# One pair of heads of the first batch: query by query instead of key by key, in another order of work

## The chip, the cores and the metric

The program runs on one core of a Trainium2 chip. The metric is the time of one execution in microseconds (us) on the device; of several executions the median is given. A profiled execution adds a trace: every instruction of the five engines (PE for matmuls, with PEld for its weight loads; DVE, ACT and POOL for element-wise work; SP, which issues the DMA transfers), with its start and duration.

## The reference

Clustered attention feeds a layer with a rational activation. A query may attend to a key only where both have the same nearest of 16 centroids; the mask is exact, so the assignment has to be as well.

```python
B, H, S, D = q.shape                       # 4, 8, 768, 64
q_assign = np.argmax(np.einsum('bhsd,hcd->bhsc', q_n, c_n), axis=-1)
k_assign = np.argmax(np.einsum('bhsd,hcd->bhsc', k_n, c_n), axis=-1)
mask = q_assign[:, :, :, None] == k_assign[:, :, None, :]
scores = np.where(mask, scale * np.matmul(q, k.transpose(0, 1, 3, 2)), -1000000000.0)
attn = np.exp(scores - np.max(scores, axis=-1, keepdims=True))
attn = attn / (np.sum(attn, axis=-1, keepdims=True) + 1e-09)
x = np.matmul(attn, v)                     # to [3072, 512]: tokens by heads
h = x @ w_in                               # 512 -> 2048
P = a[0] + a[1] * h + a[2] * h * h + a[3] * h * h * h
Q = 1.0 + np.abs(b[0]) * np.abs(h) + np.abs(b[1]) * h * h
out = (P / (Q + 1e-6)) @ w_out             # 2048 -> 512
```

## The kernel before

Matmul operands are split into two 16-bit parts, and three products of the parts are summed; this holds for the scores, for attention times `v`, and for both matrices of the layer. The weights arrive as 64-bit numbers and are taken apart in `weights` (lines 503 to 632): ACT, DVE and POOL work on 32 chunks of 128 x 512, in the first 200 us.

The heads are done in pairs, four pairs for each of the four batches, 768 tokens in six tiles of 128. `prep` (line 883) loads `q` and `k` of a pair, scales and splits them, assigns clusters and turns the parts by DMA. Then there are two forms of attention.

*Key by key* (`attend_keys`, line 1264), for the pairs named in `KEYMAJOR`. It needs the maximum of each query's scores first: twelve score tiles (line 1286; a bank of 128 queries by 768 keys, four matmuls) are reduced on DVE to `top` (line 1295). `parts` (lines 1302 to 1312) writes the maxima, split in three, into spare rows of the second query operand, which is turned once more by DMA. Then the scores are made a second time with the keys as rows: tiles `z` (line 1330, six matmuls), from which the matmul itself has subtracted the maximum; ACT's exponential writes them to `at`. `at` is at once the right operand of attention times `v` (`px`, line 1349, in 32 bit) and of the sums (line 1355). Six small instructions for a block of 256 queries (`rw`, lines 1368 to 1400: logarithm, exponential, a Newton step, `spread` by PE at line 1383, a copy, the product) divide by the sums and round to `x`.

*Query by query* (`attend`, line 1143), for all other pairs. For each of twelve tiles of 128 queries by 768 keys: scores (line 1162, four matmuls), a scaling with minimum on DVE (line 1191), the exponential with its sum on ACT, a reciprocal on DVE (line 1210), then the two 16-bit halves `ah` on ACT and DVE (line 1222), which a DMA turns into `at` (line 1229). After two tiles of both heads 36 matmuls make `px` (line 1242), which ACT and DVE round to `x` (line 1258). These pairs need `v` in two halves, `vhi` and `vlo` (line 1138), and the rows for the mask come from a tile `marks` that is turned by DMA, with a copy of the first operand's rows beside it (lines 1026 and 1034).

The layer (`moe`, line 1410) works on blocks of 256 tokens, three for a batch: `ph` (line 1450, twelve matmuls for a column block) needs the `x` of all four pairs of the batch for that block; the rational function runs on ACT, DVE and POOL (lines 1466 to 1564), and `po` (line 1575) multiplies by `w_out`.

Score tiles lie in two banks "s", and in batch 0 every third in the bank "o", which `po` uses later.

Nothing is scheduled at run time. Every step is a numbered operation, and the list `ORDER` says in which order they are given to the engines; each engine, and SP with its DMAs, works through its own steps in that order. Numbers count the steps as the loops at the end of the kernel make them. The choice of the form is one line:

```python
KEYMAJOR = {(b, hp) for b in range(B) for hp in range(kn("km", (4, 0, 0, 0))[b])}
```

Of the kernel before, what the change touches and what calls it, by code (L numbers as in the profile page):

```python
# [57 lines left out]
K = {'mulp': 0.6, 'mulp.3': 0.0, 'a0t': 1.15, 'xn': 14, 'scp': 1, 'vsc': 0.75, 'sup0': 0, 'stk': 2, 'lop': 0, 'mgp': 0, 'rvn': 2, 'at': 3, 'vn': 3, 'ah': 5, 'sqd': 0.0, 'ed': 0.0, 'ed.3': 1.0, 'gld': 0.0, 'gld.3': 1.0, 'sqd.3': 0.0, 'ghd': 0.0, 'sua': 1.0, 'acq': 0.75, 'T1': 1, 'quick': 1}  # L58
# [188 lines left out]
def clustered_attention_moe_kernel(  # L247
# [65 lines left out]
    def kn(name, default=0.0):  # L313
        return K.get(name, default)

# [8 lines left out]
    def kshare(name, b, i):  # L324
        return share(name if f"{name}.{b}" not in K else f"{name}.{b}", i)

# [1339 lines left out]
```

## Time and profile before

| | us |
|---|---|
| median of 3 runs | 929.95 |
| lowest, highest | 928.17, 933.06 |
| the profiled execution | 932.17 |
| its span, first to last instruction | 930.4 |

| engine | busy us | share of the span | instructions |
|---|---|---|---|
| PE | 863.5 | 93% | 7705 |
| DVE | 835.6 | 90% | 1503 |
| ACT | 811.2 | 87% | 1558 |
| POOL | 729.3 | 78% | 771 |

Busy time is the time in which at least one instruction of the engine runs; where records overlap, their durations sum to more. Ends of matmuls are modelled, so a busy PE isn't PE at its peak. In a row of the trace, "128x768 f16<-128x768 f32 x144 | 129.0, 901 | 7.8 <-DVE su" means: 144 instructions of this form, 129.0 us busy, 901 ns each in the mean, and 7.8 us in which the engine was idle just before them, mostly until DVE wrote `su`.

A row of a stretch has start and end, its length, then the busy time and, in brackets, the records of PE, PEld, DVE, ACT and POOL in this order, then the mean granted clock of PE, the busy share of the 16 DMA engines and what they moved in GB/s. Where a stretch is asked for the instructions of one tile alone, an engine that has none is left out: of the three rows 5, the first (`rw`) has all five, the second (`at`) PE, PEld and ACT, the third (`rest`) DVE alone; they hold the four pairs of batch 0 together.

### The profile page before, as it was taken

How to read it: one execution, taken by the hardware profiler on the slowest of the kernel's cores; microseconds unless marked ns; L12 is line 12 of the kernel's file. 1: busy time of each engine (PE TensorE's matmuls, PEld its weight loads, DVE VectorE, ACT ScalarE, POOL GpSimd, SP SyncE). 2: the span in 40 equal slices, each digit the busy share in tenths (PEclk: the TensorE clock that was granted, in tenths of full speed). 3: DMA queues.
4: the chain of work that ended last, by engine and by line, in shares of the span. 5: the costliest groups of instructions: out<-in, count | busy, mean ns of one | idle time of the engine just before them, and what ended most of it. 6: DMA issues, size and time to landing. Idle time of an engine off the chain costs nothing.

```text
span 930.4 us, 20764 instructions
## 1 busy us (share of the span) xinstructions
PE 863.5 (93%) x7705; PEld 581.1 (62%) x7705; DVE 835.6 (90%) x1503; ACT 811.2 (87%) x1558; POOL 729.3 (78%) x771
## 2 busy tenths in 40 slices
PE   1679998988899999999989999999999999999997
PEld 1357665656566666666666766666666675777663
DVE  6789999769989999999999999999999998899986
ACT  5577697989999999999999999999999998886774
POOL 2546789988999999999989988988989996464342
PEclk9989999989999999999999999999999999999999
DMA  7995765796977899998799879896987587501000
GB/s 200 232 249 130 190 193 148 177 230 138 188 133 154 164 161 203 155 167 163 155 162 180 164 135 169 178 188 110 208 150 150 92 165 130 121 2 33 8 24 23
DMA packets 360853, 137.70 MB, mean 148 GB/s; under 512 B 335665, under 2 KB 352049, under 8 KB 360753
## 3 DMA queue, kind: packets, MB, share of 16 engines
q1 hardware_dynamic: 360752, 136.39, 72.0%
q8 instruction: 60, 0.98, 0.4%
q14 instruction: 41, 0.33, 0.1%
HBM read 41.98 MB, written 6.29 MB: 52 GB/s over the span
## 4 chain that ended last, share of the span: by engine, by line
PE 54%; DVE 19%; ACT 9%; POOL 6%; issue 6%; DMA 5%; SPq 1%; ACTq 0%; DVEq 0%; POOLq 0%
PE ph L1450 18%; PE po L1575 18%; PE s L1162 7%; PE px L1242 5%; DVE ah L1222 3%; DVE s L1191 3%; DMA rvm<-in_v_dram 2%; PE s L1286 2%; DVE t L1467 1%; DVE t L1556 1%; ACT s L395 1%; PE px L1349 1%; DVE t L1468 1%; DVE top L1295 1%; PE z L1330 1%
## 5 line engine op out<-in xcount | busy, mean ns | idle before, releaser
L1450 PE MATMUL ph<-x,win 128*128 128x256 f16 x2304 | 273.1, 273 | 6.3 <-DVE t L1468 4.7
L1450 PEld LDWEIGHTS <-win 128*128 128x128 f16 x2304 | 223.2, 98 | 55.3 <-DVE t L1468 8.6
L1575 PE MATMUL po<-wout,s 128*128 128x512 f16 x1008 | 239.3, 379 | 0.7 <-POOL s L1564 0.7
L1191 DVE TENSOR_SCALAR_CACHE_REDUCE s<-s,cc 128x768 f32<-128x768 f32 x144 | 145.9, 1017 | 15.4 <-PE s L1162 14.8
L1575 PEld LDWEIGHTS <-s 128*128 128x128 f16 x1008 | 96.4, 98 | 101.2 <-issue 2.2
L1222 DVE SCALAR_TENSOR_TENSOR ah<-s,su,ah 128x768 f16<-128x768 f32 x144 | 144.9, 1011 | 5.6 <-ACT ah L395 5.3
L395 ACT ACTIVATE ah<-s,su 128x768 f16<-128x768 f32 x144 | 129.0, 901 | 7.8 <-DVE su L1210 7.2
L395 ACT ACTIVATE s<-s,nm 128x768 f32<-128x768 f32 x144 | 126.1, 876 | 7.3 <-DVE s L1191 4.9
L1162 PE MATMUL s<-sk,sq 128*128 128x384 f16 x576 | 117.8, 329 | 8.9 <-DVE ah L1222 7.9
L1516 POOL TENSOR_TENSOR s<-s,u 128x512 f32<-128x512 f32 x84 | 114.4, 1362 | 7.0
L1538 POOL TENSOR_TENSOR s<-s,u 128x512 f32<-128x512 f32 x72 | 99.1, 1378 | 7.0 <-ACT u L395 6.7
L1515 POOL TENSOR_SCALAR s<-u,g 128x512 f32<-128x512 f32 x84 | 69.6, 829 | 36.4 <-ACT u L395 33.6
L1564 POOL TENSOR_TENSOR s<-t,s 128x512 f16<-128x512 f32 x72 | 88.1, 1226 | 8.8 <-ACT s L1560 6.8
L1162 PEld LDWEIGHTS <-sq 128*128 128x128 f16 x576 | 52.2, 98 | 53.7 <-DVE ah L1222 17.9
L1556 DVE SCALAR_TENSOR_TENSOR t<-s,t 128x512 f32<-128x512 f32 x84 | 81.8, 973 | 0.8 <-POOL s L1538 0.5
L1242 PE MATMUL px<-at,vhi 128*64 128x256 f16 x864 | 75.2, 276 | 0.0
L395 ACT ACTIVATE u<-ph,gk 128x512 f32<-128x512 f32 x84 | 57.8, 688 | 9.3 <-PE ph L1450 8.7
L1468 DVE SCALAR_TENSOR_TENSOR t<-t,gk,ph 128x512 f32<-128x512 f32 x84 | 62.8, 748 | 3.0
L395 ACT ACTIVATE t<-ph,gk 128x512 f32<-128x512 f32 x84 | 65.4, 780 | 0.0
L1467 DVE SCALAR_TENSOR_TENSOR t<-ph,gk,t 128x512 f32<-128x512 f32 x84 | 62.1, 739 | 1.1 <-ACT t L395 1.0
L1545 POOL TENSOR_TENSOR t<-t,u 128x512 f32<-128x512 f32 x43 | 57.6, 1340 | 3.6
L1242 PE MATMUL px<-at,vlo 128*64 128x256 f16 x432 | 59.7, 273 | 0.0
(232 smaller groups left out, 1751.3 us busy)
## 6 DMA issues: line engine op xcount, KB each, us to landing
rwi<-in_moe_w_in_dram SPq DMA_DIRECT2D x16, 512.0 KB, 4.1
rwo<-in_moe_w_out_dram SPq DMA_DIRECT2D x16, 512.0 KB, 4.4
rk<-in_k_dram SPq DMA_DIRECT2D x32, 192.0 KB, 3.4
rq<-in_q_dram SPq DMA_DIRECT2D x32, 192.0 KB, 3.7
rvm<-in_v_dram SPq DMA_DIRECT2D x16, 384.0 KB, 3.8
rv<-in_v_dram SPq DMA_DIRECT2D x16, 384.0 KB, 4.1
out_dram<-ob SPq DMA_DIRECT2D x24, 256.0 KB, 2.9
sk<-sk SPq DMA_DIRECT2D x12, 192.0 KB, 3.4
```

The costliest lines, as they stand in the source:

```text
L395: lambda: nc.scalar.activation(out=out(), in_=in_(), func=func, **{a: (x() if callable(x) else x) for a, x in kw.items()}),
L1162: nc.tensor.matmul(sc.ap[:, i, :SH], lhsT=st["q" + x].ap[:, j, t, :], rhs=st["k" + x].ap[:, j, ks, :].rearrange("p t c -> p (t c)"), start ...
L1191: lambda nm=nm, view=view: ts(out=view(), in0=view(), scalar1=cc.ap[:, 0:1], scalar2=None, op0=ALU.mult, op1=ALU.min, accum_out=nm.ap),
L1222: lambda part=part, view=view, su=su: stt(out=part(1), in0=view(), scalar=su.ap, in1=part(0), op0=ALU.mult, op1=ALU.subtract),
L1242: nc.tensor.matmul(px.ap[j * D : (j + 1) * D, :], lhsT=vv.ap[:, j, kt, :], rhs=at[j].ap[:, p_, kt].rearrange("p t c -> p (t c)"), start=(i ...
L1450: nc.tensor.matmul(ph.ap[:, fi * TW : (fi + 1) * TW], lhsT=win[:, wpart, c, f * P : (f + 1) * P], rhs=xs[c].ap[:, xpart], start=(i == 0), ...
L1468: stt(out=t[h].ap, in0=t[h].ap, scalar=col("a1")(), in1=ph.ap, op0=ALU.add, op1=ALU.mult)
L1516: nc.gpsimd.tensor_tensor(out=sv(), in0=sv(), in1=uv(), op=ALU.mult)
L1538: lambda uv=uv, sv=sv: nc.gpsimd.tensor_tensor(out=sv(), in0=sv(), in1=uv(), op=ALU.mult),
L1556: lambda tv=tv, sv=sv: stt(out=tv(), in0=sv(), scalar=2.0, in1=tv(), op0=ALU.subtract, op1=ALU.mult),
L1564: lambda tv=tv, g16=g16, e=(nc.vector if kshare("gld", b, i_) else nc.gpsimd): e.tensor_tensor(out=g16(1), in0=tv(), in1=g16(0), op=ALU.su ...
L1575: nc.tensor.matmul(po[ti].ap, lhsT=g16(gg)[:, c0 : c0 + P], rhs=wout[:, wpart, f, :], start=(i == 0 and f == 0), stop=(i == 2 and f == NF ...
```

## The change

K gets an entry: `km` is (3, 0, 0, 0), where the default was (4, 0, 0, 0). So three pairs of batch 0 stay key by key, and the fourth, pair (0, 3), is done query by query. `ORDER` is replaced by another permutation of now 4213 numbers (4184 before), from the first to the last line. No line of the functions differs; in the changed file each stands one line lower.

```diff
-K = {'mulp': 0.6, 'mulp.3': 0.0, 'a0t': 1.15, 'xn': 14, 'scp': 1, 'vsc': 0.75, 'sup0': 0, 'stk': 2, 'lop': 0, 'mgp': 0, 'rvn': 2, 'at': 3, 'vn': 3, 'ah': 5, 'sqd': 0.0, 'ed': 0.0, 'ed.3': 1.0, 'gld': 0.0, 'gld.3': 1.0, 'sqd.3': 0.0, 'ghd': 0.0, 'sua': 1.0, 'acq': 0.75, 'T1': 1, 'quick': 1}
+K = {'mulp': 0.6, 'mulp.3': 0.0, 'a0t': 1.15, 'xn': 14, 'scp': 1, 'vsc': 0.75, 'sup0': 0, 'stk': 2, 'lop': 0, 'mgp': 0, 'rvn': 2, 'at': 3, 'vn': 3, 'ah': 5, 'sqd': 0.0, 'ed': 0.0, 'ed.3': 1.0, 'gld': 0.0, 'gld.3': 1.0, 'sqd.3': 0.0, 'ghd': 0.0, 'sua': 1.0, 'acq': 0.75, 'T1': 1, 'quick': 1, 'km': (3, 0, 0, 0)}
 
 
 ORDER = [int(i) for i in """
-3 376 377 28 375 374 4 5 6 40 7 8 0 9 379 381 382 10 29 383 32 30 388 31 391 380 33 34 392 44 384 41 490 42
+377 3 376 28 40 375 374 4 5 6 7 8 379 9 381 29 382 32 30 383 31 41 388 44 34 33 42 391 43 380 392 46 45 384
...
 """.split()]
```

What becomes of the steps of pair (0, 3): twelve maxima, `parts`, one turn, twelve `z`, twelve exponentials, three long `px` and three times the `rw` work go; twelve times minimum, exponential, reciprocal, two halves and a turn, six short `px`, `vhi`, `vlo` and the `marks` come. In the new order the first `ph` stands at place 895 (920 before), and the last `px` of pair (0, 3) behind it (before: ahead of it).

## Rows read from the trace of the kernel before

**Rows 1.** Stretches: time, busy us and records by engine, clock, DMA share, GB/s.

```profile
0.00:135.00 135.00, 98.92 (x1089) 68.61 (x1090) 111.58 (x236) 90.87 (x161) 78.94 (x101) 0.97 0.78 194
135.00:206.30 71.30, 63.08 (x788) 44.37 (x786) 55.33 (x110) 60.18 (x120) 62.87 (x83) 0.95 0.77 198
206.30:393.00 186.70, 177.31 (x1514) 118.46 (x1515) 174.17 (x315) 180.44 (x361) 175.06 (x179) 1.00 0.83 161
393.00:593.00 200.00, 194.25 (x1702) 130.17 (x1700) 189.31 (x347) 191.77 (x381) 181.88 (x187) 1.00 0.87 160
593.00:790.00 197.00, 194.66 (x1658) 129.07 (x1657) 182.88 (x332) 187.30 (x370) 172.07 (x177) 1.00 0.83 153
790.00:930.40 140.40, 135.25 (x964) 90.43 (x963) 122.31 (x168) 100.67 (x169) 58.46 (x48) 0.99 0.15 37
```

**Rows 2.** Timeline: start us, us, what; the first matmul of `ph`.

```profile
206.26 1.48 PE L1450 MATMUL ph<-x,win 128*128 128x256 f16 x12 [0.35 <-DVE df L1073]
```

**Rows 3.** Chain that ended last, in order of time: start us, us, what.

```profile
78.96 1.39 PE z L1330 x12
80.35 2.74 PE px L1349 x24
83.09 1.49 PE px L1355 x48
...
271.86 1.40 PE po L1575 x6
...
388.89 2.09 PE px L1242 x36
```

**Rows 4.** Groups of instructions by line and form, over the whole span.

```profile
L1191 DVE TENSOR_SCALAR_CACHE_REDUCE s<-s,cc 128x768 f32<-128x768 f32 x144 | 145.9, 1017 | 15.4 <-PE s L1162 14.8
L1222 DVE SCALAR_TENSOR_TENSOR ah<-s,su,ah 128x768 f16<-128x768 f32 x144 | 144.9, 1011 | 5.6 <-ACT ah L395 5.3 <-DMA rq<-in_q_dram 0.2
L395 ACT ACTIVATE ah<-s,su 128x768 f16<-128x768 f32 x144 | 129.0, 901 | 7.8 <-DVE su L1210 7.2
L1295 DVE TENSOR_REDUCE top<-s 128x1 f32<-128x768 f32 x48 | 43.9, 946 | 3.3 <-PE s L1286 3.3
L1210 DVE RECIPROCAL su<-su 128x1 f32<-128x1 f32 x144 | 22.1, 155 | 8.4 <-ACT su L395 7.2
L1258 DVE SCALAR_TENSOR_TENSOR x<-px,x 128x256 f16<-128x256 f32 x36 | 14.8, 412 | 3.5 <-ACT x L395 3.4
L1017 DVE COPY tk<-tk 128x768 f16<-128x768 f16 x4 | 2.5, 614 | 0.0
L1017 DVE COPY tq<-tq 128x768 f16<-128x768 f16 x4 | 1.9, 478 | 0.0
```

**Rows 5.** Stretch 0 to 215 us, instructions of one tile alone: `rw`, `at`, `rest`.

```profile
0.00:215.00 215.00, 8.22 (x48) 6.36 (x48) 17.32 (x36) 17.20 (x48) 7.87 (x11) 0.97 0.77 193
0.00:215.00 215.00, 52.86 (x864) 35.43 (x864) 41.39 (x48) 0.97 0.77 193
0.00:215.00 215.00, 7.87 (x16) 0.97 0.77 193
```

**Rows 6.** Timeline of ACT in steady work, one query tile and the next.

```profile
478.19 0.87 ACT L395 ACTIVATE s<-s,nm 128x768 f32<-128x768 f32 x1
478.97 0.21 ACT L395 ACTIVATION_READ_ACCUMULATOR s<-s,nm 128x1 f32 x1
479.21 0.20 ACT L395 ACTIVATE su<-su 128x1 f32<-128x1 f32 x1
479.32 0.86 ACT L395 ACTIVATE s<-s,nm 128x768 f32<-128x768 f32 x1
```

**Rows 7.** Waits from 135 to 206 us: in total, times, longest.

```profile
PEld px L1383 <- DVE rw L1377: 4.4, 5, 2.0
```

**Rows 8.** DMA issues from 393 to 593 us, the turns of `ah`: count, us to landing.

```profile
at<-ah SPq DMA_TRANSPOSE x48, 4.1
```

**Rows 9.** A stretch of 5 us ahead of the first `ph`; columns as in rows 1.

```profile
195.00:200.00 5.00, 4.65 (x19) 2.44 (x19) 3.88 (x8) 3.98 (x11) 5.00 (x6) 0.50 0.98 219
```

361 rows, old and new, of the table ORDER are left out of this document.

## The prediction

> **What bounds the kernel now.** I read the table of stretches first [rows 1]. Its cuts are the first `ph` matmul of each batch, the start of that batch's polynomial layer; the first of all starts at 206.26 us [rows 2]. The reader is to see three regimes. Up to 206.3 us the weights are split and the first batch's attention runs; here no engine is full over the whole: ACT is busy 90.87 + 60.18 = 151 of 206 us, DVE 111.58 + 55.33 = 167, POOL 142, PE 162. From 206.3 to 790 everything is nearly full at once: ACT has 180.4 of 186.7, 191.8 of 200 and 187.3 of 197 us, PE 177.3, 194.3 and 194.7, DVE 93 to 95% of each. The tail after 790 is PE's alone (135 of 140 us). So work added on ACT or DVE costs about its own length, unless it goes into the idle time before 206 us; work taken from PE before 206 us pays only where PE holds up that part. The pair that is changed, the fourth of batch 0, ends just there: the last wait in front of the first `ph` block is on its results.
>
> **The change part by part.** The code is the same; K gets one entry and the order is another permutation, of 4213 steps in place of 4184. Pair (0, 3) loses the key-by-key form and gets the one that all pairs of batches 1 to 3 have.
>
> *PE.* The twelve score tiles stay (four matmuls each in both forms). Taken away: twelve `z` tiles of six matmuls, at 1.39 us for twelve matmuls [rows 3] 72 x 0.116 = 8.3 us; three `px` blocks, 3 x (2.74 + 1.49) = 12.7 us [rows 3]; three `spread` blocks, a twelfth of the 8.22 us of PE in `rw` each [rows 5], 2.1 us. Added: three times 36 matmuls of the other `px`, 3 x 2.09 = 6.3 us [rows 3]. Net -16.8 us.
>
> *ACT.* Records of this engine overlap: the exponential, 0.87 us long, is followed by its accumulator's record 0.78 us after its start, that one by the next after 0.24, `su` by the next after 0.11 [rows 6]. So I cost by starts: 0.78 + 0.24 + 0.11 for these, and 0.81 for `ah` (901 ns in the rows [rows 4], less the same 0.09), 1.94 us for a tile at most; where another instruction stands between accumulator and `su`, some 0.1 less; I take 1.85. Twelve tiles are 22.2 us; `vhi`, an instruction of the form of `ah`, adds 0.8. The three roundings of `x` stand in both forms. Taken away: twelve `at`, a quarter of 41.39 us [rows 5], 10.3, or 9.3 less the overlap; and of the work in `rw`, a quarter of 17.20 us [rows 5], 4.3, all but the rounding of `x`, so some 3. Net +10.3 us, between +9 and +11.5.
>
> *DVE.* Added: 12 x (1.017 + 0.155 + 1.011) = 26.2 us [rows 4], the accumulator's record between 0 and the 0.24 of ACT's (I take 0.1: 1.2), and 3 x 0.41 for `x` [rows 4], 28.6. Taken away: 12 x 0.946 for the maxima, two copies, 0.61 and 0.48 [rows 4], a quarter of 7.87 for the split of the maxima [rows 5] with one write more in front of it, and a quarter of 17.32 in `rw` [rows 5]: 11.4 + 1.1 + 2.5 + 4.3 = 19.3. Net +9 us, +8 with the overlap of records on the added side.
>
> *POOL* swaps like for like (marks, `vlo` and the scaling of `rv` against fixed rows, two writes of masks and three subtractions for `x`); I take 0; its 142 of 206 us before the cut cover a microsecond either way.
>
> *DMA and SP.* Twelve turns of `ah`, two of the marks and two copies come in, three turns go. SP issues them in its own order: a turn waits there for DVE's `ah`, and behind it stand the loads of the last weights and of batch 1. A turn lands 4.1 us after its issue [rows 8], the upper bound of its price; the stretch from 393 to 593 us keeps the DMA engines busy 0.87 of 200 us [rows 1] and holds 48 such turns [rows 8] beside other transfers, so one takes 3.6 us of the engines at most. Eleven more are under 40 us; before the cut the engines are idle a quarter of the time [rows 1], 50 us. I take no delay, and keep one as a rival.
>
> **Where it lies.** Read from the two permutations: ahead of the first `ph` matmul the new order keeps as much DVE and ACT work as the old. All twelve new exponentials and all but one of the other new DVE halves stand there, but 14 other ACT instructions that stood ahead of it now stand behind: twelve of batches 1 and 2 (squares of `v`, most of the first two tiles of pair (1, 0)) and two of the weights. By the rows of their kinds ACT has 2.5 us more ahead of the cut, DVE 1.5 more, PE 22 less, POOL 10 less (three weight subtractions and a `vlo` moved behind). Between the cut and batch 1's first `ph` ACT has 22 records more (18 instructions, four accumulators); at this stretch's own mean of 180.44 us for 361 records [rows 1] they are 11 us, and I take 10.5. After that ACT has 2 us less, and PE one block of six `po` matmuls less (1.40 us [rows 3]); from batch 2 on all is equal.
>
> *First stretch.* From 135 to 206.3 us ACT is busy 60.2 of 71.3 us, DVE 55.3, PE 63.1, POOL 62.9 [rows 1]. Nothing closes up: +2.5. ACT packs as densely as in the next stretch (96.6%): (60.2 + 2.5) / 0.966 = 64.9, which is -6.4. All of ACT's idle time closes: -8.6. I take -4, nearer to the dense end: PE and POOL, the two fullest here, lose work, and the waits around `rw` (PE waited 4.4 us for DVE there [rows 7]) fall to nine blocks from twelve. The first `ph` then starts at 202.
>
> *Second stretch.* ACT has 6.3 us idle of 186.7 and DVE 12.5; +10.5 of work makes +10.5 us at the same density, +4.2 if ACT's idle time fills up. I take +10.5: there was the same reason to fill it before. *After it* PE is 97 to 99% busy [rows 1], so only its block counts, -1.4. Sum: -4 + 10.5 - 1.4 = +5.1 us. The profiled execution takes 932.17 us with a span of 930.4; a span of 935.5 is 937.3 there, and 935 against the median of 929.95, which is what is predicted.
>
> *A rule against the change.* PE gets less to do ahead of the first `ph`. The rows show a stretch of 5 us there, 195 to 200, at a granted 0.50, the level of 1.2 GHz, with 19 matmuls begun in it [rows 9]; over the two parts ahead of the first `ph` the mean is 0.97 and 0.95, from there on 1.00, the level of 2.4 GHz [rows 1]. The Trainium skill, TensorE: Matmul & The Clock Gate, Part 1, says that the halved clock is the default and that activity releases it; the trace agrees. One more such stretch would cost 2.5 us of PE where PE is late, and I add nothing, since ACT is what is late there. *And one for it:* on the turns the Trainium skill, Advanced Engine Details and Errata, X-Bar Transpose (TRN2), expects 350 to 400 GB/s, an estimated 1.0 to 1.1 us for the 393 KB of one; by that eleven turns are 12 us, and the rival of the late turns falls away. The bound from the rows, 3.6 us, doesn't exclude it.
>
> **The rivals.** *The start closes up* (faster). PE and POOL are what holds the stretch before the cut; both are relieved, its last chain (`z`, `at`, `px`, `rw`, `spread`, `x`) is gone, and `ph` needs only the first third of the pair's queries. Then the cut falls by all of ACT's idle time, -8.6, and ACT fills up behind it, +4.2: with -1.4 some -6 us, 924. For it: PE 63.1 and POOL 62.9 are the highest of that stretch. Against: DVE and ACT keep all their work, and stand at 92 to 99% in the second. It decides from a first `ph` before about 198 us. *It cancels out*: the first stretch packs to the dense end, -6.4, and 2.5 of ACT's idle 6.3 us in the second fill, +8: with -1.4 it is 930. For it: the sum is of terms of opposite sign, neither known better than 4 us. *The turns are late* (slower): SP's queue and the DMA engines are full from 150 to 205 us, and the first query blocks of the pair wait for their turned `ah`. With 3.6 us a turn, eleven take 40 of the some 50 us that the engines are idle before the cut, and a share of these lies before the pair begins. Two turns late one behind the other, 4.1 us each, on the way from the pair's first three tiles of queries to their `x`, put +8 on the sum: 943. Against: at a price of 2 us a turn there is room for all, and the loads of batch 1 can wait. It decides from a DMA share of 1.0 before the cut.
>
> **How the numbers follow.** My forecast, 935, with its own range 931 to 940, gets 0.45; the cancelling 0.21; the closing up 0.20; the late turns 0.14. A difference of 0.5%, 4.65 us, is about what can be told from none here. The forecast's part under 934.6 is a third of its chance, so that "same" is 0.15 + 0.21 = 0.36, slower 0.30 + 0.14 = 0.44, faster 0.20. The range takes in the closing up, 923, and the late turns, 943.
>
> **What would show it.** In the profile of the changed kernel ACT should be busy some 10 us longer (821.5) and DVE 8 (843.5), PE 12 to 17 us less; the first `ph` at 198 to 205 us; from there to batch 1's first `ph` 195 to 198 us with ACT at 96% or more; and then the same 537 us to the end but for a microsecond. A first `ph` before 198, or a second stretch under 191 us, makes the forecast wrong to the fast side; a DMA share near 1 from 150 to 205 us with PE waiting on `at`, to the slow side. If the stretch after batch 1's first `ph` changes by more than 3 us, the new order did something there that this sum doesn't hold.

## The result, and the profile after

The changed kernel takes 939.22 us (median; 938.88 to 940.12), the kernel before, run on the same chip, 929.06 us: a ratio of 1.0106, with a 95% interval of 1.007 to 1.0141. It is 10 us slower; 935 was forecast, the sign of the sum was right and its size half of what came.

The profiled execution of the changed kernel took 938.88 us, with a span of 937.1. That is 6.7 us more than the span before [rows 1]. The difference from 10 us lies in the execution before: its 932.17 us were some 3 us above the median of its own kernel, those of the changed one were not above theirs.

The busy time of the engines over the whole span, from the first part of the page of the changed kernel:

```profile
PE 856.6 (91%) x7510; PEld 575.5 (61%) x7510; DVE 854.9 (91%) x1525; ACT 821.4 (88%) x1586; POOL 733.2 (78%) x768
```

and of the kernel before:

```profile
PE 863.5 (93%) x7705; PEld 581.1 (62%) x7705; DVE 835.6 (90%) x1503; ACT 811.2 (87%) x1558; POOL 729.3 (78%) x771
```

ACT has 10.2 us more, as the sum said; DVE has 19.3 more, where 8 were forecast. The table of stretches of the changed kernel, cut at its own first `ph` matmuls of each batch, answers to [rows 1] and has the same columns:

```profile
0.00:135.00 135.00, 97.47 (x1038) 68.35 (x1042) 114.27 (x232) 90.36 (x162) 83.53 (x99) 0.94 0.74 193
135.00:198.70 63.70, 47.90 (x543) 32.87 (x531) 57.15 (x122) 61.58 (x129) 53.67 (x72) 0.87 1.01 228
198.70:394.90 196.20, 186.48 (x1630) 124.98 (x1629) 184.46 (x333) 190.62 (x382) 184.18 (x190) 0.99 0.94 177
394.90:595.50 200.60, 193.92 (x1696) 129.72 (x1695) 188.47 (x343) 190.21 (x378) 180.71 (x187) 1.00 0.85 160
595.50:794.20 198.70, 194.85 (x1657) 129.44 (x1656) 187.91 (x331) 188.23 (x370) 172.16 (x176) 1.00 0.83 149
794.20:937.10 142.90, 135.96 (x966) 90.14 (x963) 122.66 (x169) 100.34 (x169) 58.94 (x48) 1.00 0.17 38
```

The reader is to see four things. The first `ph` comes at 198.7 us, 7.6 earlier than at [rows 2]. The second stretch is 196.2 us where it was 186.7, and not ACT alone grew in it: PE 186.5 from 177.3, DVE 184.5 from 174.2, ACT 190.6 from 180.4, POOL 184.2 from 175.1, each by 9 to 10 us. The stretches behind it are longer as well, by 0.6, 1.6 and 2.5 us, although ACT's and PE's time there hardly changed. And the DMA share ahead of the first `ph` is 1.01, the condition that the rival of the late turns named.

Cut at the first `ph` of each batch, with two of the experiments beside them (us; the cuts of the kernel before are here the exact ones, a little off the round ones of [rows 1]):

| kernel | to batch 0 | to batch 1 | to batch 2 | to batch 3 | to the end |
|---|---|---|---|---|---|
| before | 206.3 | 186.6 | 200.0 | 197.1 | 140.4 |
| after | 198.7 | 196.2 | 200.6 | 198.7 | 142.9 |
| new start, old rest | 199.2 | 196.2 | 199.7 | 197.0 | 140.7 |
| old start, new rest | 205.5 | 187.8 | 202.0 | 198.8 | 142.7 |

### The profile page after: what moved, and what is told of

It is laid out like the page before. It is cut to its first block, busy times and chain, and to the rows that moved or that the text cites. A ratio compares the mean times of both kernels' runs of the same rounds, so it can differ in the third digit from the quotient of the medians.

```text
span 937.1 us, 20427 instructions
## 1 busy us (share of the span) xinstructions
PE 856.6 (91%) x7510; PEld 575.5 (61%) x7510; DVE 854.9 (91%) x1525; ACT 821.4 (88%) x1586; POOL 733.2 (78%) x768
## 4 chain that ended last, share of the span: by engine, by line
PE 42%; DVE 26%; ACT 13%; issue 8%; POOL 6%; DMA 4%; SPq 0%; ACTq 0%; DVEq 0%; POOLq 0%
PE po L1576 13%; PE ph L1451 13%; PE s L1163 6%; PE px L1243 5%; DVE s L1192 5%; DVE ah L1223 5%; ACT s L396 3%; DVE top L1296 2%; ACT ah L396 2%; DVE t L1557 2%; DVE t L1468 2%; PE z L1331 2%; ACT u L396 2%; DVE t L1469 1%; DMA rwo<-in_moe_w_out_dram 1%
## 5 line engine op out<-in xcount | busy, mean ns | idle before, releaser
L1192 DVE TENSOR_SCALAR_CACHE_REDUCE s<-s,cc 128x768 f32<-128x768 f32 x156 | 157.8, 1017 | 12.3 <-PE s L1163 11.6
L1223 DVE SCALAR_TENSOR_TENSOR ah<-s,su,ah 128x768 f16<-128x768 f32 x156 | 156.3, 1009 | 4.2 <-ACT ah L396 3.7
L1163 PE MATMUL s<-sk,sq 128*128 128x384 f16 x624 | 130.6, 335 | 22.0 <-DVE ah L1223 19.3
L396 ACT ACTIVATE ah<-s,su 128x768 f16<-128x768 f32 x156 | 139.2, 899 | 12.0 <-DVE su L1211 10.9
L396 ACT ACTIVATE s<-s,nm 128x768 f32<-128x768 f32 x156 | 136.4, 875 | 10.6 <-DVE s L1192 7.4
L1163 PEld LDWEIGHTS <-sq 128*128 128x128 f16 x624 | 57.2, 99 | 73.3 <-DVE ah L1223 30.9
L1516 POOL TENSOR_SCALAR s<-u,g 128x512 f32<-128x512 f32 x84 | 73.4, 873 | 36.8 <-ACT u L396 33.5
L1243 PE MATMUL px<-at,vhi 128*64 128x256 f16 x936 | 82.1, 277 | 2.8 <-DVE t L1469 1.4
L1557 DVE SCALAR_TENSOR_TENSOR t<-s,t 128x512 f32<-128x512 f32 x84 | 82.4, 981 | 1.4 <-POOL s L1539 0.8
L1243 PE MATMUL px<-at,vlo 128*64 128x256 f16 x468 | 65.2, 275 | 0.0
L1468 DVE SCALAR_TENSOR_TENSOR t<-ph,gk,t 128x512 f32<-128x512 f32 x84 | 62.1, 739 | 0.4 <-ACT t L396 0.3
L1243 PEld LDWEIGHTS <-vhi 128*64 128x64 f16 x936 | 48.1, 110 | 22.8 <-issue 15.2
```

The costliest lines, as they stand in the source:

```text
L396: lambda: nc.scalar.activation(out=out(), in_=in_(), func=func, **{a: (x() if callable(x) else x) for a, x in kw.items()}),
L1163: nc.tensor.matmul(sc.ap[:, i, :SH], lhsT=st["q" + x].ap[:, j, t, :], rhs=st["k" + x].ap[:, j, ks, :].rearrange("p t c -> p (t c)"), start ...
L1192: lambda nm=nm, view=view: ts(out=view(), in0=view(), scalar1=cc.ap[:, 0:1], scalar2=None, op0=ALU.mult, op1=ALU.min, accum_out=nm.ap),
L1223: lambda part=part, view=view, su=su: stt(out=part(1), in0=view(), scalar=su.ap, in1=part(0), op0=ALU.mult, op1=ALU.subtract),
L1243: nc.tensor.matmul(px.ap[j * D : (j + 1) * D, :], lhsT=vv.ap[:, j, kt, :], rhs=at[j].ap[:, p_, kt].rearrange("p t c -> p (t c)"), start=(i ...
L1468: stt(out=t[h].ap, in0=ph.ap, scalar=col("rho")(), in1=t[h].ap, op0=ALU.mult, op1=ALU.mult)
```

## The experiments

### The start and the rest of the order, apart

The change has two parts that the diff shows as one list: the pair (0, 3) in its new form with a new order around it, and another order of the later batches, whose steps are the same. Two kernels hold one part each: their list of steps is that of one kernel up to batch 1's first `ph` and from there on takes the steps that are left in the order of the other. The edit is in `ORDER` alone. For the new start with the old rest, the numbers of the list at the seam (its first 1861 stay):

```diff
...
 1794 1798 1225 1240
-1861 1795 1799 1226 1241 1796 1809 1800 1845 1801
+2554 1845 2296 1795 1799 1788 1226 1214 1800 1801
...
```

The new start with the old rest. Expected:

> The changed kernel; but all steps from the first ph of batch 1 on stand in the order of the kernel before. In the two profiles the changed kernel is 2.0 us behind at this ph and 6.7 us at the end, so 4.7 us arise after it, where both do the same work. Theory, the other order of the later batches costs these 4.7 us: span near 932.5, time 934 to 935 where the changed kernel has 939. Rival, the later loss is inherited from the start (from the state of buffers and loads that the pair leaves): no gain, 939.

Measured: 933.93 us (932.65 to 935.6) against 929.56, a ratio of 1.004 [1.0024, 1.0056].

The old start with the new rest. Expected:

> The kernel before; but all steps from the first ph of batch 1 on stand in the order of the changed kernel. Theory, the later order costs by itself: 4 to 5 us slower than before, 933 to 934. Rival, inherited from the start: as before, 929.

Measured: 935.75 us (933.37 to 938.54), a ratio of 1.0068 [1.0049, 1.0087]. The two add up: +4.4 and +6.2 are 10.6, the whole change was 10.2. In the table above the new start with the old rest has, stretch by stretch and within 0.5 us, the times of the kernel whose order it follows there; so has the old start with the new rest, within 0.8, but for the two stretches at its seam, 187.8 and 202.0 us where the two kernels that it joins have 186.6 and 200.6. So the larger half of the loss, by the medians, has nothing to do with the pair: the other order of the steps from batch 1's first `ph` on costs it, with the same steps.

The last two stretches go with the order alone. In the eleven profiles of this document with the changed kernel's order there they take 198.7 to 198.9 and 142.6 to 142.9 us, in the three with the order of before 197.0 to 197.1 and 140.4 to 140.7, whatever stands ahead of them. These are some 4 us of the loss.

The stretch from batch 1's first `ph` to batch 2's of the kernel before, as in the table of stretches:

```profile
392.90:592.90 200.00, 194.25 (x1701) 130.19 (x1700) 189.31 (x347) 191.77 (x381) 181.88 (x187) 1.00 0.87 160
```

PE's two longest waits for DVE in it (us in total, times, longest):

```profile
PEld L1162 <- DVE ah L1222: 7.7, 8, 2.6
...
PE s L1162 <- DVE ah L1222: 4.9, 6, 2.1
```

The same stretch of the old start with the new rest:

```profile
393.30:595.30 202.00, 194.05 (x1696) 129.65 (x1695) 190.51 (x344) 191.64 (x380) 180.51 (x187) 1.00 0.86 160
```

and the same waits in it (the lines of this kernel are eight lower):

```profile
PEld L1154 <- DVE ah L1214: 11.1, 15, 1.8
...
PE s L1154 <- DVE ah L1214: 5.8, 8, 1.3
```

And in that stretch of the changed kernel, 200.6 us long:

```profile
PEld L1163 <- DVE ah L1223: 9.3, 13, 1.8
...
PE s L1163 <- DVE ah L1223: 4.3, 8, 1.3
```

The counts of records are nearly the same, 1701 and 1696 matmuls, 347 and 344 of DVE, 381 and 380 of ACT; the time is 2.0 us longer, and the score tiles wait 16.9 us in place of 12.6 for DVE's `ah` (PE and its weight loads together, in part at the same time). But the changed kernel waits 13.6 us there, hardly more than before, and most of its loss lies in the two stretches behind. So these waits don't account for the loss. That the order costs it was tried; through which waits was not, and stays open. (The profiled execution of the old start with the new rest, 938.54 us, is also the longest of its ten.)

### Form and order, apart

Expected of the new form of the pair, with all else in the order of before:

> The new form of pair (0, 3), with all other steps in the order of the kernel before; the pair's new steps are put among the neighbours that they have in the changed kernel. Theory, the pair's own work on ACT and DVE (10 and 8 us more) has no room: 5 us slower than before, 934, with the first ph later or the stretch behind it longer. Rival, the form is free and only the order costs: 929 to 930. An order that was patched like this can be worse than either: over 940 would tell that it was.

Measured: 973.0 us, a ratio of 1.046 [1.0422, 1.0498]. Expected of the old form in the new order:

> The old form of pair (0, 3), with all other steps in the order of the changed kernel; the pair's old steps are put among the neighbours that they have in the kernel before. Theory, form and order each cost about half: 934. Rival 1, all is the form's: 929. Rival 2, all is the order's: 939.

Measured: 986.3 us, 1.0605 [1.0564, 1.0646]. The edits are the entry `km` and the list, in which the pair's steps are put among their neighbours and others are moved so that all dependencies hold. Both orders are patches, and the time they lose at the patch covers what was asked: in the first, the first `ph` starts only at 242.9 us. They tell nothing of form against order in the new start, whose 4.4 us stay undivided, except that a form put into an order made for another one took 43 and 57 us more than the kernel before.

### What holds the second stretch

The sum put +10.5 us into the second stretch because ACT gets so much more and is nearly full. If ACT holds it, ACT's time there can also be taken out again. Four kernels, each the changed one with work of one engine left out of batch 0's polynomial, which lies in that stretch:

```diff
...
-                act((630, 1070)[k], uv, uv, AF.Exp, [], us, uu + kb("ln", b), [u_t], scale=-1.0)
+                if b or i_ % 6 == 5:
+                    act((630, 1070)[k], uv, uv, AF.Exp, [], us, uu + kb("ln", b), [u_t], scale=-1.0)
+                else:
+                    op("ACT", 0, lambda: None, [], us, uu + kb("ln", b), [u_t])
...
-                    lambda tv=tv, sv=sv: stt(out=tv(), in0=sv(), scalar=2.0, in1=tv(), op0=ALU.subtract, op1=ALU.mult),
+                    lambda tv=tv, sv=sv, skip=b == 0 and i_ % 2: None if skip else stt(out=tv(), in0=sv(), scalar=2.0, in1=tv(), op0=ALU.subtract, op1=ALU.mult),
...
-                        lambda uv=uv, sv=sv: nc.gpsimd.tensor_tensor(out=sv(), in0=sv(), in1=uv(), op=ALU.mult),
+                        lambda uv=uv, sv=sv, skip=b == 0 and i_ % 12 in (0, 2, 5, 7, 10): None if skip else nc.gpsimd.tensor_tensor(out=sv(), in0=sv(), in1=uv(), op=ALU.mult),
...
                         for wpart, xpart in ((0, 0), (0, 1), (1, 0)):
+                            if b == 0 and c in (1, 2) and xpart:
+                                i += 1
+                                continue
...
```

Expected of less ACT work:

> The changed kernel with less ACT work in batch 0's polynomial, which lies in the second stretch (198.7 to 394.9 us of its trace): 20 of the 24 exponentials behind the logarithm are left out (their results stay logarithms), 20 x 0.632 us = 12.6 us of ACT. Theory (ACT holds this stretch, as the step for +10.5 us said): the stretch gets 9 to 12 us shorter and the time is 927 to 930 us against 939.2. Rival (several engines hold it in turn, so that ACT alone brings little): 934 to 938 us.

Of less DVE work:

> The changed kernel with less DVE work in the same stretch: the last product of the polynomial (t = (s - 2) t) is left out for 12 of batch 0's 24 pieces, 12 x 1.048 us = 12.6 us of DVE. Theory (ACT holds the stretch): 0 to -3 us, 936 to 939 us. Rival (DVE holds it, with 184 of 196 us busy and score tiles that wait for its ah): -8 to -12 us, 927 to 931 us.

Of less POOL work:

> The changed kernel with less POOL work in the same stretch: 10 of batch 0's 24 products s = s u are left out, 10 x 1.322 us = 13.2 us of POOL. Theory (ACT holds the stretch): 0 to -3 us, 936 to 939 us. Rival (POOL and DVE slow each other, so that less of POOL makes the DVE instructions shorter): DVE's records of the stretch shorter by 3% or more in their means, and -5 us or more, under 934 us.

Of less PE work:

> The changed kernel with less PE work in the same stretch: 2 of the 12 matmuls of each of batch 0's 48 ph halves are left out (a low-order product), 96 x 0.122 us (70.2 us for 577 in the rows) = 11.7 us of PE. Theory (ACT holds the stretch): 0 to -3 us, 936 to 939 us. Rival (PE, busy 186 of 196 us, is the bound there too): -6 to -11 us, 928 to 933 us.

Measured: 939.08 us (937.96 to 940.14), 936.9 (935.99 to 937.1), 939.74 (939.09 to 940.4) and 938.43 (937.59 to 938.82), against 939.22. The kernel before, run beside these four, took 930.67 us, and 929.06 beside the changed kernel; so a microsecond or two between their medians tells little, and the stretches have to speak. The second stretch of each, from its own first `ph` to batch 1's; with less ACT work:

```profile
198.00:394.30 196.30, 186.25 (x1630) 124.81 (x1629) 183.95 (x333) 182.81 (x362) 184.17 (x190) 0.99 0.93 177
```

With less DVE work:

```profile
198.40:392.70 194.30, 183.52 (x1629) 124.17 (x1628) 176.17 (x324) 190.66 (x383) 180.50 (x191) 1.00 0.95 181
```

With less POOL work:

```profile
199.30:395.10 195.80, 185.88 (x1630) 125.18 (x1629) 180.50 (x333) 190.20 (x383) 169.63 (x180) 0.99 0.94 178
```

With less PE work:

```profile
198.00:393.30 195.30, 180.65 (x1534) 116.91 (x1533) 182.10 (x331) 189.55 (x381) 184.91 (x190) 0.97 0.90 179
```

The theory falls. With 20 records less ACT is busy 182.8 us in place of 190.6 (7.8 less and not 12.6, since its records overlap [rows 6]), and the stretch stays at 196.3. The other three give 1.9, 0.4 and 0.9 us, as small as the theory had them, but the theory stood on ACT. ACT simply waits longer, and for DVE. Two groups of ACT in this stretch of the changed kernel (busy us, mean ns, idle time before and what ended it):

```profile
L396 ACT ACTIVATE ah<-s,su 128x768 f16<-128x768 f32 x43 | 38.4, 900 | 1.7 <-DVE su L1211 1.5
L396 ACT ACTIVATE s<-s,nm 128x768 f32<-128x768 f32 x43 | 37.7, 877 | 1.2 <-DVE s L1192 0.9
```

The same groups with less ACT work:

```profile
L396 ACT ACTIVATE ah<-s,su 128x768 f16<-128x768 f32 x43 | 38.3, 897 | 4.7 <-DVE su L1211 4.4
L396 ACT ACTIVATE s<-s,nm 128x768 f32<-128x768 f32 x43 | 37.6, 873 | 3.2 <-DVE s L1192 3.0
```

The rivals that DVE or PE is the one bound fall too; the one of POOL is taken up at the end, its time didn't come either. What was left is that all four hold the stretch at once, or none. A kernel with all four omissions together tells these apart. Expected:

> All four omissions together in batch 0's polynomial: 20 exponentials on ACT (12.6 us), 12 last products on DVE (12.6), 10 products on POOL (13.2), 96 matmuls on PE (11.7). One at a time they brought 0.1, 2.3, -0.5 and 0.8 us. Theory (the second stretch is held by all four engines at once, each 94 to 97% full): the stretch of 196.2 us gets 8 to 12 us shorter, the time is 927 to 931. Rival (none of the four holds it, but the transfers or the way the score tiles pass from engine to engine): at most 4 us less, 935 or more.

Measured: 932.77 us (931.42 to 935.54), a ratio of 1.0042 [1.0027, 1.0057] to the kernel before. Its second stretch:

```profile
201.50:390.70 189.20, 174.20 (x1533) 114.36 (x1532) 169.64 (x322) 181.06 (x363) 168.58 (x181) 1.00 0.95 184
```

189.2 us, 7.0 less than 196.2; the four one at a time had given 3.1 in sum. That is nearer to the theory's 8 to 12 than to the rival's 4, but short of it, and the time lies between the theory's 927 to 931 and the rival's 935. ACT is busy 9.6 us less in the stretch, PE 12.3, DVE 14.8 and POOL 15.6, so 3 to 9 us of that turned into waiting. Its first `ph` was 2.8 us later than the changed kernel's, with the same steps ahead of it; why is open, and in the other kernels that keep these steps it lies between 198.0 and 199.3. Some of the 7.0 us may belong to that: batch 1's first `ph` comes 4.2 us earlier, and the median is 6.4 lower. Whether it takes all four engines, or two or three of them would do, was not tried.

The other thing that was full in this stretch are the DMA engines. Half of each turn of batch 1 left out:

```diff
-                        out=at[j].ap.rearrange("p s k t c -> p (s k) t c")[:, :, ti, :],
-                        in_=ah.ap.rearrange("p s k -> p (s k)"),
+                        out=at[j].ap.rearrange("p s k t c -> p (s k) t c")[:, : NT if b == 1 else 2 * NT, ti, :],
+                        in_=ah.ap.rearrange("p s k -> p (s k)")[:, : S if b == 1 else 2 * S],
...
-                            rhs=at[j].ap[:, p_, kt].rearrange("p t c -> p (t c)"),
+                            rhs=at[j].ap[:, 0 if b == 1 else p_, kt].rearrange("p t c -> p (t c)"),
```

Expected:

> The changed kernel with half of each of batch 1's 48 turns left out (the low-order part; its matmuls take the high part instead), all in the second and third stretch: 48 x 196 KB less for the DMA engines, whose share in the second stretch is 0.94. Theory (the engines hold the stretch together): within 1.5 us of 939.2. Rival (the DMA engines hold it): 5 us or more less, 934 or under.

Measured: 938.81 us (938.16 to 939.75). The second stretch:

```profile
198.40:394.50 196.10, 186.24 (x1629) 125.01 (x1628) 184.41 (x333) 190.57 (x382) 184.09 (x190) 0.99 0.71 137
```

The share fell from 0.94 to 0.71, a turn landed 3.1 us after its issue in the median in place of 4.3, and the stretch stayed within 0.1 us. The transfers don't hold it.

### The turns ahead of the first `ph`

The rival of the late turns was to decide from a DMA share of 1.0 there, and 1.01 came. Two kernels ask what it costs. One adds a transfer of the size of a turn behind each of the pair's twelve:

```diff
...
+                        n == "0_3" and nc.sync.dma_start(
+                            out=out[S + 192 * (2 * (tb * TB + ti) + j) :][:192].rearrange("r (c d) -> (r c) d", c=4).rearrange("(p a) d -> p a d", a=6),
+                            in_=ah.ap.rearrange("p s k -> p (s k)").bitcast(F32).rearrange("p (a d) -> p a d", a=6),
+                        ),
...
```

Expected:

> The changed kernel with twelve transfers more on SP's queue: behind each turn of the changed pair (159 to 200 us) the same ah tile, 393 KB, is also stored to rows of the output that are overwritten much later. At the stretch's 228 GB/s twelve are some 21 us of the DMA engines, where their share is 1.01 already. Theory (the turns of the pair are on nobody's path): the first ph stays within 1.5 us of 198.7 and the time within 2 us of 939.2. Rival (the turns are late: the full DMA engines hold the stretch before the first ph): the first ph comes 5 us or more later, with PE waiting on at, and the time is 943 or more.

Measured: 945.77 us (944.48 to 947.15), 6.6 more than the changed kernel; the first `ph` came at 202.8, 4.1 later. The theory's 1.5 and 2 us are passed; the rival has its time, but not its 5 us at the first `ph`. The chain of waits (start us, us, what) ahead of the first `ph` has these transfers on it:

```profile
145.93 5.46 DMA rwi<-in_moe_w_in_dram
...
167.71 4.90 DMA rwo<-in_moe_w_out_dram
...
177.49 4.50 DMA rvm<-in_v_dram
```

where the chain of the changed kernel has one:

```profile
164.30 3.81 DMA at<-ah
```

PE has no wait for `at` there. So it isn't `at` that comes late but the loads that stand behind in the queue, two of weights and one of `v`. An added store also keeps its `ah` tile longer, so that not all of the 4.1 us need be the queue's. The other kernel takes half of each of the pair's turns away; the edit is that of batch 1's turns with the pair `0_3` as its condition. Expected:

> The changed kernel with half of each of the changed pair's twelve turns left out (the low-order part; its matmuls take the high part instead): 12 x 196 KB less for the DMA engines between 159 and 203 us, where their share is 1.01 (at 228 GB/s some 10 us of them). All other work stays. Theory (these turns are on nobody's path, as the prediction's sum has it): first ph within 1 us of 198.7 and the time within 1.5 us of 939.2. Rival (the DMA engines hold that stretch, so that loads which stand behind the turns come late): first ph 2 us or more earlier and the time 937 or under.

Measured: 938.53 us (937.91 to 939.92), 0.7 less than the changed kernel; the first `ph` at 197.5. The last stretch ahead of it:

```profile
135.00:197.50 62.50, 46.41 (x502) 31.35 (x500) 57.19 (x121) 60.12 (x126) 52.80 (x71) 0.87 0.89 204
```

With a share of 0.89 in place of 1.01 there is 1.2 us at the first `ph`, a little outside the theory's 1 and short of the rival's 2; the other kernels with these steps have 198.0 to 199.3, the 201.5 above aside. In the median there is 0.7, within the theory's 1.5. Half of the pair's turns cost a microsecond or so at most; what the whole of them costs was not tried, and there was no room left for as many again.

## Why the prediction came out as it did

**First stretch, -4: mis-sized, -7.6.** The mechanism fits what came: the last chain of the key-by-key form goes, and ACT closes up. The dense end of the sum said 64.9 us for the part from 135 us on, and 63.7 came, with ACT at 61.58 of 63.7, 96.7%, the density taken from the next stretch; the rest of the difference is that ACT has 1.4 us more there and not 2.5. I took a value between this end and no gain at all; the row said the dense end. DVE didn't stand against packing so close: over 45 us, from 155 to 200, it is busy 43.1 us and ACT 43.2. That ACT, and not DVE, sets the pace there was not tried. (The first part says that the last wait in front of the first `ph` is on the pair's results; [rows 2] name another, 0.35 us for DVE's `df` of line 1073.)

**The clock, nothing.** The granted clock of the last part ahead of the first `ph` is 0.87 where it was 0.95 [rows 1], so more of it ran at the level of 1.2 GHz, and yet the first `ph` came earlier: PE is busy 47.9 of 63.7 us there and is not what is late.

**Second stretch, +10.5: right in size (+9.6), wrong in its reason.** ACT has the 10.2 us that were counted. But I had priced only ACT there, and PE, DVE and POOL gained as much, since the first `ph` comes earlier and what had stood beside the pair's end now stands behind it. The prediction's own counts had some of that behind the cut, some 10 us of POOL, 6.5 of DVE's 8 and 5 of PE, and put no price on it. Less ACT work alone brings nothing, less of all four brings 7.0 us. The sentence in the first part, that everything is nearly full at once, was right; that added work on ACT "costs about its own length" is not shown by the 9.6 us, because the other engines had the same length added here.

**After it, -1.4: this step failed.** The sum had the same 537 us to the end, since the work of the later batches is the same. The stretch from batch 1's first `ph` to the end is 937.1 - 394.9 = 542.2 us; before it was 537.5. In the kernel with the old rest it is 932.8 - 395.4 = 537.4, in that with the new rest 936.8 - 393.3 = 543.5. Equal work was taken as equal time, though the list of these steps was permuted too. The last sentence of the prediction names this sign, a change of over 3 us there, but no term had a price for it: none of the rivals has a new order of the same steps in a full stretch as its mechanism, and that was worth 5 to 6 us.

**DVE, +8: mis-sized, +19.3.** With the old rest DVE has 847.6 us, 12.0 more than before; with the old start and the new rest 841.3, 5.7 more, with the same 1503 records. So about 12 go with the start, 6 with the order of the same steps. The sum took the durations of the rows before for fixed; on DVE they depend on what runs beside them (below).

**PE, -16.8: -6.9 over the whole.** Ahead of the first `ph` it is -16.6 (145.4 from 162.0), where -22 was read from the lists. PE's records are pipelined, more of them ran at the lower clock (0.94 and 0.87 in the two parts ahead of it, 0.97 and 0.95 before), and its busy time is not a sum of matmuls; nothing hung on this term.

**The step to the median.** 5.1 us were added to a profiled execution that lay at the high end of its kernel, and the sum was then carried to the median by its own offset. Against its own span the result is +6.7, near the forecast's 5.1, with errors of -3.6, -0.9 and +6.1 in the three stretches that in part cancel: that the sum came near is luck. Against the medians it is +10.2. The 3.5 us between the two are nearly all the profiled execution's place within its own spread (927 to 933 us).

**The rivals.** The start closing up was to decide from a first `ph` before 198 us and a second stretch under 191; neither came. The cancelling needed ACT's idle time in the second stretch to fill, and ACT is idle 5.6 us there, as before (6.3). Up to batch 1's first `ph` its -6.4 + 8 = +1.6 was still nearer than the forecast's +6.5 in the profiles (394.9 from 392.9, +2.0); by the medians the new start costs 4.4, between the two. The late turns came with their sign, the share of 1.01, and without their wait: halving them is worth a microsecond or so. The time lies nearest to theirs, 943, by another mechanism.

## What to carry to other kernels

Where the order is written out by hand or by a planner, price the order itself: two lists of the same steps differed by 5 to 6 us in 540 here, more than the 4.4 of the new start with the form that was to be judged in it; cut the list at a seam and take either part alone before an edit inside it is judged. In a stretch where four engines were 94 to 97% busy, work taken from the fullest alone returned nothing, and from all four 7.0 us; so ask of an addition what the other engines get in the same stretch. Take the idle time ahead of such a stretch for what a row of the next stretch says of it, not for the middle of the possible; here it was the row that came.

## What the runs showed of the hardware

Some DVE instructions have no fixed duration: the same ones, on the same shape, got shorter or longer by up to a fifth with the work around them, while others kept theirs. In the second stretch, groups of DVE (busy, mean ns, idle before) of the changed kernel:

```profile
L1223 DVE SCALAR_TENSOR_TENSOR ah<-s,su,ah 128x768 f16<-128x768 f32 x44 | 44.1, 1009 | 2.1 <-ACT ah L396 1.7
...
L1557 DVE SCALAR_TENSOR_TENSOR t<-s,t 128x512 f32<-128x512 f32 x22 | 23.1, 1048 | 0.1
...
L1468 DVE SCALAR_TENSOR_TENSOR t<-ph,gk,t 128x512 f32<-128x512 f32 x24 | 17.8, 741 | 0.4 <-ACT t L396 0.3
L1552 DVE SCALAR_TENSOR_TENSOR t<-t,gk,u 128x512 f32<-128x512 f32 x9 | 12.4, 1374 | 0.0
```

and of the kernel with ten POOL products less:

```profile
L1223 DVE SCALAR_TENSOR_TENSOR ah<-s,su,ah 128x768 f16<-128x768 f32 x43 | 43.0, 1009 | 2.4 <-ACT ah L396 2.2
...
L1557 DVE SCALAR_TENSOR_TENSOR t<-s,t 128x512 f32<-128x512 f32 x22 | 21.8, 991 | 0.0
...
L1468 DVE SCALAR_TENSOR_TENSOR t<-ph,gk,t 128x512 f32<-128x512 f32 x24 | 17.8, 741 | 0.3 <-ACT t L396 0.2
L1552 DVE SCALAR_TENSOR_TENSOR t<-t,gk,u 128x512 f32<-128x512 f32 x9 | 10.1, 1127 | 0.0
```

The same operation on the same shape takes 741 ns in L1468, and 1374 or 1127 in L1552; the first and L1223 have one tile operand in PSUM (`ph`, `s`) and don't change, the other two have both in SBUF and do. All 333 DVE records of the stretch together went from 184.46 to 180.50 us, 2%, short of the 3% that the rival for that run wanted, with the time unchanged.

The ten POOL products are not all of it. With all of POOL's work in place the group of L1552 has a mean of 1211 ns with less ACT work and 1218 with less PE work, that of L1557 1076 and 1023. And from batch 2's first `ph` to batch 3's DVE's busy time grew by 4.9 us with POOL as busy as before (172.07 and 172.16 us) and only the order changed. Before:

```profile
L1556 DVE SCALAR_TENSOR_TENSOR t<-s,t 128x512 f32<-128x512 f32 x25 | 23.2, 928 | 0.1
...
L1551 DVE SCALAR_TENSOR_TENSOR t<-t,gk,u 128x512 f32<-128x512 f32 x10 | 11.1, 1111 | 0.0
```

After:

```profile
L1557 DVE SCALAR_TENSOR_TENSOR t<-s,t 128x512 f32<-128x512 f32 x25 | 25.2, 1007 | 0.1
...
L1552 DVE SCALAR_TENSOR_TENSOR t<-t,gk,u 128x512 f32<-128x512 f32 x10 | 12.4, 1237 | 0.0
```

The Trainium skill, SBUF — State Buffer, section "SBUF: two separate sides", says that a DVE operation with two SBUF inputs and a GpSimd (POOL) operation that reads SBUF lock each other out of a shared port for a whole instruction. These rows agree with that in which groups change; that it is POOL's instructions that hold them up was not tried apart from the order. So a duration of such a DVE group belongs to an order of work, and the sum's DVE term could not be read from the rows before alone. Whether these longer DVE instructions are what the later stretches lost their time by was not tried.
